# One tile's residual moved from a vector add to an accumulating transfer of GpSimd, in a hand-ordered end of an attention kernel

## The chip, the cores and the metric

The kernel runs on one core of one Trainium2 chip. The metric is the device time of one execution in microseconds (us). The engines are named as the profile names them: PE (matrix multiplications), DVE (VectorE), ACT (ScalarE), POOL (GpSimd) and SP (SyncE, which here only issues transfers).

## The reference

```python
def reference(A_x, A_wq, A_wk, A_wv, A_wo, B_x, B_w1, B_w2):
    x = A_x                                   # (1, 2048, 512), bfloat16
    xn = _layernorm(x, axis=-1)
    s = _A_ref(xn, A_wq, A_wk, A_wv, A_wo)    # attention, 32 query heads of 16, one k/v head; output projection wo
    g = _silu(_B_ref(xn, B_w1, B_w2))         # dense 512 -> 1792, silu, dense 1792 -> 512
    return x + s * g
```

## The kernel before

The 2048 rows are cut into four chunks of 512, and the 32 heads into groups of four, which makes 32 groups in order, eight to a chunk. For each group PE forms scores (line 643, and line 692 for the last group's parts) in PSUM banks psA, psD and psF. The exponential of some tiles is taken on ACT (`exp_A`, line 674, from psA to `pa_sb`), and of others as integer arithmetic on DVE (line 714) with shifted copies made by POOL with an int64 add (line 739). PE then multiplies both with v into psO (`emit_quad`, line 769): four matmuls over four column strips, a "quad". The feed-forward branch g is worked out in between and kept in `tmp_sb`.

The order of the instructions is written out by hand as two strings. `ORDER` is for the bulk. `TAIL`, read by `finish`, is for the end of the last group. A helper, `Sched`, puts each operation into its engine's queue in the order of the string, and derives the semaphore waits from the names of what it reads and writes. So a letter's place decides where an instruction stands in the queue of its own engine; letters of different engines that change places change nothing.

The last group's output for a few key blocks is worked out in three parts of its 512 rows: part 0 has rows 0 to 255, part 1 has 256 to 383, part 2 has 384 to 511. The letters of `TAIL`:

- `H`: eight (or four) score matmuls of one part on PE and their exponential on ACT
- `v`, and `q` with a part: one quad of PV on PE
- `n` with a part: the next of the part's four normalising steps on DVE: transpose from psO (line 920), reciprocal (923), product (872), transpose into `xn_sb` (929)
- `P`: four matmuls of the output projection of the next of the last chunk's four row tiles (line 404), for head groups that are already done; three to a tile, and the banks of tiles 0 to 3 are psF, the two halves of psD, and psA
- `r` with a tile: the last four matmuls of that projection, which need the part of the tile's rows (part 0 for tiles 0 and 1, part 1 for tile 2, part 2 for tile 3)
- `G`: bank times g on DVE, from PSUM (line 1429); or in two steps `C`, a copy on ACT out of PSUM (line 1424), and `M`, the product on DVE from SBUF (line 1426)
- `A`: the residual, an add of x on DVE into `ob_sb` (line 1444), and a store on SP's queue
- `X`, `Y`: the residual on PE by the identity matrix (line 1435); `Z`: its copy on ACT into `ob_sb` (line 1439) and a store on ACT's queue
- `a`: the residual by an accumulating transfer on POOL's queue, which adds the tile to the output in memory:

```python
op("gp", lambda e: e.dma_start(ov[:, tt, :], src, accum_op=ALU.add), reads=[key, "outx"], writes=[("out", tt)],
   lane=f"ac{tt % 4}", cost=3.0)
```

The output holds x already: one transfer copies all of it there early (line 397, `outx`). The tiles of the first three chunks are finished with such accumulating transfers (twelve in all, line 1122). At the start of `finish` POOL is given a small add on `mhalf_sb` (line 1398), before which its configuration is changed. At the end SP waits for all stores.

Of the kernel before, what the change touches and what calls it, by code (L numbers as in the profile page):

```python
# [213 lines left out]
def bass_recurrent_scan__grouped_kv_mqa__dense_activation_silu__prompt_kernel(  # L214
# [84 lines left out]
    TAIL = "vvHvvHvvHvvHq0q0q0q0q1q1q1q1n0PPn1Pn0n1q2q2q2q2n0Pn1n0Pn1Pn2r0r1C1n2G0PPPn2r2A0Pn2PM1PG2r3X1Y1Z1G3A2A3"  # L299
    ALPHA = "".join(chr(x) for x in range(35, 127) if x != 92) + "".join(chr(x) for x in range(192, 255))  # L300

    with ExitStack() as es:
# [1206 lines left out]
        while not followed:  # L1509
# [71 lines left out]
            else:  # L1581
                now = 0.0
        finish(TAIL)
        last = {}
# [36 lines left out]
```

## Time and profile before

| | us |
|---|---|
| median of 3 runs | 637.72 |
| lowest and highest run | 637.59, 638.5 |
| the profiled execution | 637.56 |
| its span | 635.8 |

The profile shows one execution. A row of the timeline gives the start in us from the span's start, the length in us, the engine, the line, the operation, output<-inputs and shapes, xN for N merged instructions, and in brackets how long the engine was idle before and what released it. PEld is PE's load of weights. For a transfer, the row's length is that of its issue; the time from issue to landing is given separately. The span's last 2.5 us show no instruction of a compute engine, only transfers.

### The profile page before, as it was taken

The numbers are of one execution on the slowest core, as the hardware profiler recorded it, in microseconds if no ns is written. First come the engines' busy times: TensorE is split into PE (matmuls) and PEld (weight loads), VectorE is DVE, ScalarE is ACT, GpSimd is POOL, SyncE is SP. The second block draws the span as 40 slices with busy tenths as digits, with TensorE's granted clock in tenths as the row PEclk, the third lists the DMA queues.
The fourth block names the chain that finished last, engine by engine and source line by source line (L and its number), as shares of the span: only waits on it lengthen the run. The fifth ranks groups of instructions, "written<-read, shape, count | busy, mean of one in ns | idle before, by whom it ended". The sixth has DMA issues, their size and how long they took to land.

```text
span 635.8 us, 18802 instructions
## 1 busy us (share of the span) xinstructions
PE 628.9 (99%) x8225; PEld 195.9 (31%) x8227; DVE 605.6 (95%) x1049; ACT 625.3 (98%) x721; POOL 436.4 (69%) x438
## 2 busy tenths in 40 slices
PE   8999999999999999999999999999999999999997
PEld 3433333332323222223223332223323233223323
DVE  7999999999999999999999999999999999999994
ACT  8999999999999999999999999999999999999996
POOL 6466665767667778767666876678767776776771
PEclk9999999999999999999999999999999999999999
DMA  6380000000000100000000000001000000000012
GB/s 183 119 283 2 2 2 2 2 3 1 2 2 2 19 1 11 10 2 2 1 3 2 1 3 2 2 10 18 10 3 2 2 2 1 3 1 2 3 18 53
DMA packets 10083, 12.51 MB, mean 20 GB/s; under 512 B 2288, under 2 KB 9456, under 8 KB 9968
## 3 DMA queue, kind: packets, MB, share of 16 engines
q1 hardware_dynamic: 7840, 9.34, 4.5%
q0 software_dynamic: 1728, 1.57, 2.2%
q8 instruction: 64, 1.05, 0.7%
q10 hardware_dynamic: 432, 0.39, 0.2%
q14 instruction: 19, 0.16, 0.1%
HBM read 8.95 MB, written 4.19 MB: 21 GB/s over the span
## 4 chain that ended last, share of the span: by engine, by line
PE 84%; ACT 9%; DVE 5%; issue 0%; DMA 0%; DVEq 0%
PE psO L769 32%; PE psA L643 27%; PE psF L404 20%; ACT pa_sb L674 8%; DVE ph_sb L714 3%; PE psD L643 2%; DVE x_sb L714 1%; ACT t_sb L1116 0%; PE psA L692 0%; DMA x_sb<-in_A_x_dram 0%; PE psD L507 0%; PE psD L476 0%; PE psF L643 0%; PE psD L533 0%; DVE stats_sb L424 0%
## 5 line engine op out<-in xcount | busy, mean ns | idle before, releaser
L674 ACT ACTIVATE pa_sb<-psA 128x1024 bf16<-128x1024 f32 x630 | 593.0, 1078 | 1.7 <-PE psA L643 0.6
L739 POOL INT64_ADD ph_sb<-ph_sb x304 | 317.1, 1058 | 131.0 <-DVE ph_sb L714 130.8
L714 DVE TENSOR_SCALAR ph_sb<-psD 128x512 int16<-128x512 f32 x521 | 336.3, 681 | 10.4 <-PE psD L643 8.5
L769 PE MATMUL psO<-ph_sb,vaug_sb 128*32 128x512 bf16 x1824 | 227.7, 383 | 0.1
L769 PE MATMUL psO<-pa_sb,vaug_sb 128*32 128x512 bf16 (+1 forms) x1292 | 201.6, 378 | 0.2 <-DVE rcp_sb L923 0.2
L643 PE MATMUL psA<-qT_sb,kTa_sb 32*128 32x512 bf16 x632 | 122.1, 384 | 0.1
L739 POOL INT64_ADD x_sb<-x_sb x90 | 93.5, 1057 | 41.4 <-DVE x_sb L714 41.3
L643 PE MATMUL psA<-qT_sb,kTb_sb 32*128 32x512 bf16 x612 | 118.4, 385 | 0.3 <-ACT pa_sb L674 0.3
L643 PE MATMUL psD<-qT_sb,kTb_sb 32*128 32x512 bf16 x335 | 113.5, 384 | 0.0
L643 PE MATMUL psD<-qT_sb,kTa_sb 32*128 32x512 bf16 x339 | 110.8, 385 | 0.0
L714 DVE TENSOR_SCALAR x_sb<-psD 128x512 int16<-128x512 f32 x153 | 100.7, 682 | 6.1 <-PE psD L643 5.3
L769 PE MATMUL psO<-x_sb,vaug_sb 128*32 128x512 bf16 x540 | 96.4, 383 | 0.0
L769 PEld LDWEIGHTS psO<-ph_sb,vaug_sb 128*32 128x32 bf16 x1824 | 55.6, 95 | 57.5 <-issue 35.1
L643 PEld LDWEIGHTS psA<-qT_sb,kTa_sb 32*128 32x128 bf16 x632 | 29.7, 91 | 122.0 <-ACT pa_sb L674 93.1
L404 PE MATMUL psF<-w_sb,u_sb 128*32 128x512 bf16 x896 | 66.2, 384 | 0.0
L643 PEld LDWEIGHTS psA<-qT_sb,kTb_sb 32*128 32x128 bf16 x612 | 28.7, 91 | 121.1 <-ACT pa_sb L674 99.2
L404 PE MATMUL psF<-xnT_sb,w_sb 128*32 128x512 bf16 x896 | 64.7, 383 | 0.0
L769 PEld LDWEIGHTS psO<-pa_sb,vaug_sb 128*32 128x32 bf16 x1292 | 50.2, 95 | 33.7 <-issue 24.2
L714 DVE TENSOR_SCALAR ph_sb<-psF 128x512 int16<-128x512 f32 x70 | 47.6, 680 | 0.0
L1116 ACT ACTIVATE t_sb<-psF 128x512 bf16<-128x512 f32 x72 | 46.3, 643 | 0.0
L1135 DVE SCALAR_TENSOR_TENSOR u_sb<-t_sb,psF 128x512 bf16<-128x512 bf16 x56 | 38.0, 678 | 0.2
L643 PEld LDWEIGHTS psD<-qT_sb,kTa_sb 32*128 32x128 bf16 x339 | 28.8, 91 | 2.2 <-DVE ph_sb L714 0.4
(120 smaller groups left out, 396.1 us busy)
## 6 DMA issues: line engine op xcount, KB each, us to landing
w_sb<-in_B_w_dram SPq DMA_DIRECT2D x2, 1792.0 KB, 10.9
x_sb<-in_A_x_dram SPq DMA_DIRECT2D x3, 512.0 KB, 5.6
out_dram<-ob_sb POOLq DMA_DIRECT2D x12, 128.0 KB, 3.1
wop_sb<-in_A_wo_dram SPq DMA_DIRECT2D x1, 512.0 KB, 4.0
wq_sb<-in_A_wq_dram SPq DMA_DIRECT2D x1, 384.0 KB, 5.9
out_dram<-ob_sb SPq DMA_DIRECT2D x3, 128.0 KB, 1.9
x_sb<-in_A_x_dram SPq DMA_DIRECT2D x2, 128.0 KB, 2.7
x_sb<-in_A_x_dram ACTq DMA_DIRECT2D x2, 128.0 KB, 2.9
```

Of the source, the lines that this page charges most:

```text
L404: r = e.matmul(bank[32 * i:32 * i + 32, :], lhsT=w, rhs=rhs, start=start, stop=stop, tile_position=(0, 32 * i), skip_group_check=True)
L643: return e.matmul(ap, lhsT=kT_sb[g % 2][32 * i:32 * i + 32, kt * P:(kt + 1) * P], rhs=qT_sb[32 * i:32 * i + 32, c % 2, g // 2, :], start=T ...
L674: d = op("a", lambda e: e.activation(pa_sb[:, sl, :], psA[k][:, :], ACT.Exp, scale=ESCALE), reads=["A%d" % k], writes=[("pa", sl)], cost=2 ...
L714: d = op("v", lambda e: e.tensor_scalar(ph_ap(0, sl, 512 * pos, 512 * pos + m), src, float(PH_ONE + PH_BIAS), 0.0, op0=ALU.add, op1=ALU.ma ...
L739: d = op("gp", lambda e, j=j: e.int64_add(ph_ap(j, sl, 0, 4 * NQ).bitcast(I64), ph_ap(0, sl, 0, 4 * NQ).bitcast(I64), PH_SHIFT[j] * 0x0001 ...
L769: r = e.matmul(psO[32 * i:32 * i + 32, cs], lhsT=vaug_sb[:, p["v"], p["kt"], DH * (gi % 2):DH * (gi % 2) + 32], rhs=p["ap"], start=s0, sto ...
L1116: d = op("a", lambda e: e.activation(t_sb[:, n % 2, :], bank_ap(b), ACT.Tanh, scale=0.5 if jb[0] == "h" else 0.25), reads=[b], writes=[("t ...
L1135: op("v", lambda e: e.scalar_tensor_tensor(out=dst, in0=t_sb[:, n % 2, :], scalar=1.0, in1=src, op0=ALU.add, op1=ALU.mult), reads=tk["read ...
```

## The change

The one string `TAIL` is replaced. Tile 0's residual was `A0` (add on DVE, store on SP) and is now `a0`, the accumulating transfer on POOL, from the scaled tile itself (`wq_sb`, whose space holds it by then). Tile 3's product with g was `G3` and is now `C3` and `M3`. The letters around them are in another order:

```diff
-    TAIL = "vvHvvHvvHvvHq0q0q0q0q1q1q1q1n0PPn1Pn0n1q2q2q2q2n0Pn1n0Pn1Pn2r0r1C1n2G0PPPn2r2A0Pn2PM1PG2r3X1Y1Z1G3A2A3"
+    TAIL = "vvHvvHPvvvvHHq0q0q0q0q1q1q1q1n0PPn1PPn0Pn1Pq2q2q2n0n1q2Pn0n1r1n2C1n2n2Pr2Pn2r0PPr3X1G2C3M1A2G0a0Y1M3Z1A3"
```

By engine, the queues before and after differ as follows from the second H on:

- PE: one P and four v stand between the second and third H, which is then followed at once by the fourth; six P instead of three stand between the quads of part 1 and those of part 2; after these it is P, r1, P, r2, P, r0, PP, r3, X1, Y1 instead of PPP, r0, r1, PPP, r2, PPP, r3, X1, Y1.
- DVE, after step 1 of part 2: step 2, step 3, G2, M1, A2, G0, M3, A3 instead of G0, step 2, A0, step 3, M1, G2, G3, A2, A3.
- ACT: C3 is added between C1 and Z1.
- POOL: the accumulating transfer of tile 0 is added behind the add on `mhalf_sb`, as the last entry of the queue.
- SP: two stores instead of three; the last is that of tile 3 in both.

## The prediction

> **What bounds the kernel now.** I read the page's head first, then the chain of waits that ended last, cut to its last microseconds, then the timeline of each engine there, and last the sources of the two kinds of transfer to the output.
>
> ```profile
> span 635.8 us, 18802 instructions
> PE 628.9 (99%) x8225; PEld 195.9 (31%) x8227; DVE 605.6 (95%) x1049; ACT 625.3 (98%) x721; POOL 436.4 (69%) x438
> ```
>
> PE, ACT and DVE are busy for nearly the whole span, and an edit of the tail string touches none of that: until the second of the last four H, at 624.63, both kernels issue the same instructions in the same order. Only the last 11 us can move, so a fault in my sum is a fraction of a microsecond, not a per cent.
>
> ```profile
> 626.86 0.80 PE psO L769 x32
> 628.48 0.41 PE psO L769 x16
> 629.80 0.04 DVE wq_sb L1429
> 632.55 0.41 DVE ob_sb L1444
> 632.95 0.34 DVEq L302
> ```
>
> These pieces (start, length, what) show the chain leaving PE when the last quads of part 2 are done (628.48 + 0.41 = 628.89), and running on DVE from there until the last residual add. What DVE does in that stretch is this, from its timeline (start, length, line, output<-inputs):
>
> ```profile
> 628.80 0.44 DVE L929 STREAM_TRANSPOSE xn_sb<-onb_sb 128x128 f32<-128x128 f32 x2
> 629.16 0.27 DVE L920 STREAM_TRANSPOSE otr_sb<-psO 128x128 f32<-128x128 f32 x1
> 629.47 0.18 DVE L923 RECIPROCAL rcp_sb<-otr_sb 128x4 f32<-128x4 f32 x1
> 629.80 0.69 DVE L1429 SCALAR_TENSOR_TENSOR wq_sb<-psF,tmp_sb 128x512 bf16<-128x512 f32 x1 [0.15 <-PE psF L404]
> 630.41 0.22 DVE L872 TENSOR_TENSOR onb_sb<-otr_sb,rcp_sb 128x64 bf16<-128x64 f32 x1
> 630.54 0.42 DVE L1444 TENSOR_TENSOR ob_sb<-wq_sb,x_sb 128x512 bf16<-128x512 bf16 x1
> 630.88 0.23 DVE L929 STREAM_TRANSPOSE xn_sb<-onb_sb 128x64 f32<-128x64 f32 x1
> 631.04 0.38 DVE L1426 TENSOR_TENSOR wq_sb<-wq_sb,tmp_sb 128x512 bf16<-128x512 bf16 x1
> 631.35 0.68 DVE L1429 SCALAR_TENSOR_TENSOR wq_sb<-psD,tmp_sb 128x512 bf16<-128x512 f32 x1
> 631.95 0.67 DVE L1429 SCALAR_TENSOR_TENSOR wq_sb<-psA,tmp_sb 128x512 bf16<-128x512 f32 x1
> 632.55 0.74 DVE L1444 TENSOR_TENSOR ob_sb<-wq_sb,x_sb 128x512 bf16<-128x512 bf16 x2
> ```
>
> From 629.80 to 632.55 + 0.74 = 633.29 DVE has no gap: G0, step 2 and A0, step 3, M1, G2, G3, A2, A3 in the letters of the string. What follows is the store of tile 3 on SP, read from the timeline and from the store's source:
>
> ```profile
> 632.98 0.82 SPq L1391 DMA_DIRECT2D out_dram<-ob_sb  x2
> L1391 SPq DMA_DIRECT2D out_dram<-ob_sb x2: 350/390/431, 633.0 to 633.4; - x2
> ```
>
> The last issue ends at 632.98 + 0.82 = 633.80 and took 0.43, so it began at 633.37, 0.08 after the add.
>
> **Part 1: part 2's scores are issued later (costs).** The new string puts one output projection (P) and four quads (v) between the second and the third of the four H, and the third and fourth H together.
>
> ```profile
> 624.28 0.38 PE L769 MATMUL psO<-pa_sb,vaug_sb 128*32 128x512 bf16 x1
> 624.63 0.40 PE L692 MATMUL psA<-qT_sb,kTb_sb 32*128 32x128 bf16 x8
> 624.96 0.39 PE L769 MATMUL psO<-ph_sb,vaug_sb 128*32 128x512 bf16 x1
> 625.18 0.38 PE L769 MATMUL psO<-pa_sb,vaug_sb 128*32 128x512 bf16 x1
> 625.55 0.40 PE L692 MATMUL psA<-qT_sb,kTb_sb 32*128 32x128 bf16 x8
> 626.47 0.40 PE L692 MATMUL psA<-qT_sb,kTb_sb 32*128 32x128 bf16 x8
> 627.00 1.25 ACT L674 ACTIVATE pa_sb<-psA 128x1024 bf16<-128x1024 f32 x1
> 586.38 1.94 ACT L674 ACTIVATE pa_sb<-psA 128x1024 bf16<-128x1024 f32 x2 [0.25 <-PE psD L643]
> ```
>
> Four column matmuls take 0.22 (624.96 to 625.18). Five such groups put the last at 624.96 + 4 x 0.22 = 625.84; back to scores takes 0.35 (624.28 to 624.63), so the third H starts at 626.19 instead of 625.55. Its matmuls end 0.40 later, and an exponential starts 0.13 after that (626.47 + 0.40 to 627.00): 626.72. The pair at 586.38 began on an idle ACT: 1.94 for both. So the fourth exponential ends at 626.72 + 1.94 = 628.66, where it ended at 627.00 + 1.25 = 628.25: 0.41 later. The fourth H still waits for the same exponential as before (626.47) and costs nothing more.
>
> **Part 2: PE behind it.**
>
> ```profile
> 627.46 0.82 PE L404 MATMUL psF<-wop_sb,xn_sb 128*32 128x512 bf16 x12
> 628.70 0.83 PE L404 MATMUL psD<-wop_sb,xn_sb 128*32 128x512 bf16 x12
> ```
>
> Six P instead of three now stand before the quads of part 2 (PP, PP, P, P), besides the one done already at 624.96. Six slots of 0.22 from 627.46 end at 628.78, just under the start of those quads, which is 0.23 after the exponential (628.25 to 628.48), thus 628.89. The P are therefore hidden by ACT; without that cover each would cost 0.22. The quads end at 628.89 + 0.41 = 629.30. DVE's next step used to start at 629.16 because DVE itself was busy with parts 0 and 1 until then (628.80 + 0.44 = 629.24, the steps overlap by some hundredths); now PE releases it, 0.05 after its end, at 629.35. So only 0.19 of the 0.41 reaches DVE.
>
> **Part 3: DVE is relieved (gains).** Part 2's four steps go first, each waiting for the one before with 0.03 between them: 629.35, 629.66, 629.87, 630.12, ending at 630.35 where they ended at 630.88 + 0.23 = 631.11. Then, by the start-to-start times of the rows above (0.16 after a step 3, 0.60 after a G, 0.31 after M1, 0.34 after an A): G2 630.28, M1 630.88, A2 631.19, G0 631.53, M3 632.13. A3 needs M3's result, 0.38 + 0.03 later: 632.54, ending 632.95. That is 0.34 before the old end: A0 has gone (0.34), G3 (0.60) has become M3 (0.41), against 0.19 lost at the start and the waits that nothing fills now.
> PE has the banks in time: after the quads P 629.11, r1 629.33, P 629.55, r2 629.77, which ends at 630.18, before G2; P, r0 at 630.21, long before G0; PP and r3 at 630.87, ending 631.28. The added copy C3 on ACT has the row of C1:
>
> ```profile
> 630.01 0.60 ACT L1424 ACTIVATE wq_sb<-psD 128x512 bf16<-128x512 f32 x1 [1.77 <-PE psD L404]
> ```
>
> 631.34 + 0.60 = 631.94, 0.19 before M3. Behind C3 on ACT wait Z1 and the store of tile 1; Y1, which waits for M1's end at 631.26, started 0.43 after it before, so Z1 starts near 632.1 and its store lands near 634.5, not last. SP loses one store and keeps A2's and A3's; A3's is issued at 632.95 + 0.08 = 633.03.
>
> **Part 4: the accumulating transfer (costs).** It replaces A0 and a store on SP. It is the last entry of POOL's queue, behind the add on mhalf; nothing waits behind it but the end.
>
> ```profile
> L1122 POOL DMA_DIRECT2D out_dram<-ob_sb x12: 850/869/1165, 210.5 to 622.5; - x12
> DMA to landing us min/median/max: 2.8/3.1/3.4
> DMA to landing us min/median/max: 1.9/2.0/2.0
> 421.20 0.68 DVE L1147 SCALAR_TENSOR_TENSOR ob_sb<-psF,tmp_sb 128x512 bf16<-128x512 f32 x1
> 422.18 0.87 POOL L1122 DMA_DIRECT2D out_dram<-ob_sb  x1 [1.20 <-DVE ob_sb L1147]
> 630.49 0.19 POOL L1398 TENSOR_TENSOR mhalf_sb<-mhalf_sb 128x4 f32<-128x4 f32 x1 [7.09 <-issue]
> 633.30:635.80 2.50, 0.00 (x0) 0.00 (x0) 0.00 (x0) 0.00 (x0) 0.00 (x0) 0.93 0.45 157
> ```
>
> The first landing row is the accumulate's, the second that of the last two plain stores. POOL starts 0.30 after DVE's result (421.20 + 0.68 to 422.18), and is free since 630.68. G0 ends at 631.53 + 0.68 = 632.21, so the transfer is issued at 632.51 and lands at 635.61 by the median of twelve (635.3 to 635.9 by their ends). It shares the DMA engines with A3's store. The end of before moved 157 GB/s at a share of 0.45, so about 350 GB/s when full (my estimate from that row); 128 KB are 0.37 us. Sharing costs between nothing and that; three plain stores overlapped in the old end without landing later than 2.0, so I take the low side, 0.1: landed at 635.71.
> The old end was 633.37 + 1.95 = 635.32, with 0.44 to the span's end at 635.76. A3's store would now land at 633.03 + 1.95 = 634.98, and the accumulate 0.7 after it. **Sum:** -0.34 on the old last store, then +0.73 because another transfer is last: 635.71 + 0.44 = 636.15, that is +0.4. The profiled execution took 637.56 outside and all; it becomes 637.96. The median before, 637.72, lies 0.16 above that execution, so the median after is **638.1**. About 0.2% (1.28 us) is what a measurement of this kernel can tell from no change, so this is a "same".
>
> **Rivals.**
> *Hidden transfer.* The accumulate lands before A3's store, which then sets the end: -0.34, 637.4. It decides from a landing time of 634.98 - 632.51 = 2.47 down; the fastest of twelve took 2.8, so against. The Trainium skill, "DMA: Bandwidth & Descriptors", section "Anatomy of one DMA — SWDGE (gpsimd) path", fits 2.0 us plus bytes over 436 GB/s for such a transfer, by which 128 KB would take about 2.3 us and this rival would win; the trace disagrees with its 3.1.
> *Locked out by DVE.* M3 and A3 run from 632.13 to 632.95, over the issue. If POOL can write nothing before A3 ends, the issue slips by 632.95 - 632.51 = 0.44, and the median after is 638.5; with a landing of 3.4 and full sharing it is 639.1. One old issue did overlap a DVE operation with two inputs:
>
> ```profile
> 454.20 0.73 DVE L872 TENSOR_TENSOR onb_sb<-otr_sb,rcp_sb 128x512 bf16<-128x512 f32 x1
> 454.58 0.88 POOL L1122 DMA_DIRECT2D out_dram<-ob_sb  x1 [0.52 <-DVE ob_sb L1147]
> ```
>
> It took 0.88 against 0.87, so against; but its inputs were f32, not bf16. The Trainium skill, "SBUF — State Buffer", section "SBUF: two separate sides", warns that DVE's two-port modes starve the descriptors of GpSimd's transfers; its section "Who interferes with whom" excepts tensor_tensor. By the warning this rival holds, by the exception my sum.
> *POOL not ready (slower).* All twelve old accumulates were issued between int64 adds. This one comes after POOL's change of configuration, which kept it for 7.09 us until 630.49. If the transfer needs such a change again, it starts at 630.68, ends at 637.77, and the landing comes at 640.9: the span ends at 641.3, a median of 643.3. It decides from 0.9 us of extra delay, where the result passes +0.2%. Against it: the first accumulate, at 210.5, came in the middle of adds and shows no such gap, only an issue of 1.17 at most.
>
> **How the numbers follow.** My forecast has 0.60, the hidden transfer 0.12, the lockout 0.14, POOL not ready 0.14 (with any long first start there). The range runs from the hidden transfer, less 0.1 for the spread of the runs, 637.3, to the lockout's upper end, 639.2; it leaves out POOL not ready. Slower by over 0.2% (over 639.0) has that 0.14, a third of the lockout, and 0.04 of the forecast where landing and sharing are both at their worst and H comes later than I have it: 0.23. Faster by over 0.2% would need a landing before 634.0, which no case reaches; 0.04 for what I have not seen. The same: 0.73.
>
> **What would show it.** In the new profile: the last L674 ending near 628.65; L929 of part 2 ending near 630.35; the last L1444 near 632.95; a POOL L1122 starting near 632.5 and landing near 635.7, last of all. It is wrong if SP's last wait is for the plain store, if the POOL row starts late, or if DVE shows a gap before the second L1426 (then C3 was late).

## The result, and the profile after

| us | before | after |
|---|---|---|
| median of 21 runs each, side by side | 638.42 | 639.40 |
| lowest and highest | 637.50, 639.37 | 638.33, 640.82 |
| the profiled execution | 637.56 | 639.53 |
| its span | 635.8 | 637.7 |

The ratio is 1.0016, with a 95% interval of 1.0009 to 1.0022: the changed kernel is slower by about 1.0 us. The middle value is within 0.2%, but the whole interval lies above 1, and the loss is about 2.5 times the 0.4 us forecast. The 639.4 also lies above the range, whose upper end was 639.2. Part of that has nothing to do with the change: the median of before is 638.42 over 21 runs, 0.70 above the 637.72 of three runs that the prediction started from. On that base the measured +0.98 would have given 638.70, inside the range.

The profiled executions differ by 1.97 us, and half of this is not in the end at all. These are the `L692` rows of the first of the last four H before, and of the first and second in the changed kernel:

```profile
623.72 0.40 PE L692 MATMUL psA<-qT_sb,kTb_sb 32*128 32x128 bf16 x8
```

```profile
624.63 0.40 PE L692 MATMUL psA<-qT_sb,kTb_sb 32*128 32x128 bf16 x8
625.55 0.40 PE L692 MATMUL psA<-qT_sb,kTb_sb 32*128 32x128 bf16 x8
```

So 0.91 us were lost ahead of any instruction that the change moves. A second profile of each kernel (last experiment) has that stretch the other way round, so it scatters between executions. Everything below is therefore read from the first of the four H. Its time to the span's end is called the tail here; ends and landings are taken from the trace to the nanosecond. The tail was 12.05 us before and is 13.10 us after, +1.05, which agrees with the medians' +0.98.

The chain of waits of the changed kernel, its last pieces (start, length, what):

```profile
630.95 0.25 DVE xn_sb L929
631.20 0.02 DVE wq_sb L1429
631.22 0.48 issue
631.69 0.40 DVE wq_sb L1426
632.10 0.33 DVE ob_sb L1444
632.43 0.61 DVE wq_sb L1429
633.04 0.29 issue
633.33 1.05 POOL out_dram L1122
```

Before, the chain ended with the last `L1444` on DVE. Now it leaves DVE after G0 (`L1429` at 632.43) and ends in POOL's issue of the accumulating transfer. The timeline of the same stretch:

```profile
627.07 0.70 PE L692 MATMUL psA<-qT_sb,kTb_sb 32*128 32x128 bf16 x16
627.51 1.94 ACT L674 ACTIVATE pa_sb<-psA 128x1024 bf16<-128x1024 f32 x2 [0.18 <-PE psA L692]
630.12 0.32 DVE L920 STREAM_TRANSPOSE otr_sb<-psO 128x128 f32<-128x128 f32 x1
630.95 0.25 DVE L929 STREAM_TRANSPOSE xn_sb<-onb_sb 128x64 f32<-128x64 f32 x1
631.12 0.65 DVE L1429 SCALAR_TENSOR_TENSOR wq_sb<-psD,tmp_sb 128x512 bf16<-128x512 f32 x1
632.35 0.69 DVE L1429 SCALAR_TENSOR_TENSOR wq_sb<-psF,tmp_sb 128x512 bf16<-128x512 f32 x1
632.95 0.42 DVE L1426 TENSOR_TENSOR wq_sb<-wq_sb,tmp_sb 128x512 bf16<-128x512 bf16 x1
633.33 1.05 POOL L1122 DMA_DIRECT2D out_dram<-wq_sb  x1 [1.55 <-DVE wq_sb L1429]
633.40 0.42 DVE L1444 TENSOR_TENSOR ob_sb<-wq_sb,x_sb 128x512 bf16<-128x512 bf16 x1
633.85 0.35 SPq L1391 DMA_DIRECT2D out_dram<-ob_sb  x1
```

DVE ends at 633.40 + 0.42 = 633.82, which is 632.91 on the scale of before (less 0.91), and 0.38 earlier than the 633.29 there. So DVE did gain. What comes after it is seen in three more views: the source of the accumulate (line 1122, its last instance), the source of the closing instructions (line 302), and SP's waits, all of the changed kernel.

```profile
L1122 POOL DMA_DIRECT2D out_dram<-wq_sb x1: 1055/1055/1055, 633.3 to 633.3; - x1
DMA to landing us min/median/max: 3.6/3.6/3.6
L302 POOLq DRAIN  x1: 3917/3917/3917, 633.6 to 633.6; - x1
L302 ACTq DRAIN  x1: 155/155/155, 633.6 to 633.6; - x1
L302 SPq DRAIN  x1: 7/7/7, 637.1 to 637.1; - x1
L302 SPq EVENT_SEMAPHORE  x1: 17/17/17, 637.7 to 637.7; - x1
SPq L302 <- DMA out_dram<-wq_sb: 0.7, 1, 0.7
SPq L302 <- PEq L302: 0.6, 1, 0.6
```

And of before, the rows that answer to them:

```profile
L302 POOLq DRAIN  x1: 10349/10349/10349, 621.4 to 621.4; - x1
L302 SPq DRAIN  x1: 7/7/7, 635.5 to 635.5; - x1
L302 SPq EVENT_SEMAPHORE  x1: 17/17/17, 635.7 to 635.7; - x1
SPq L302 <- PEq L302: 0.2, 1, 0.2
```

The transfer lands 3.60 us after its issue began, at 633.33 + 3.60 = 636.93. Then comes something that the prediction did not have. POOL's queue ends with a closing instruction, DRAIN, which every engine has. Before, it ended at 621.4 + 10.35 = 631.7, long before the end. Now it ends at 637.51, which is 0.57 after the landing. SP is done with its own DRAIN at 637.1 and then waits 0.6 us instead of 0.2 (the view names PE's queue, whose part was long done; the last DRAIN to end is POOL's). From the landing to the span's end there are 0.80 us, where before there were 0.46 from the last store's landing. So of the 1.05 us, 0.72 are the later last landing (12.30 of the tail against 11.59) and 0.34 the longer closing. Not every engine's DRAIN waits in this way: ACT's took 0.15 and was over 1.8 us ahead of the landing of ACT's own store (9.13 against 10.94 of the tail).

### The profile page after: what moved, and what is told of

It is laid out like the page before. It is cut to its first block, busy times and chain, and to the rows that moved or that the text cites. A ratio compares the mean times of both kernels' runs of the same rounds, so it can differ in the third digit from the quotient of the medians.

```text
span 637.7 us, 18802 instructions
## 1 busy us (share of the span) xinstructions
PE 630.1 (99%) x8227; PEld 196.3 (31%) x8227; DVE 606.3 (95%) x1048; ACT 626.0 (98%) x722; POOL 436.2 (68%) x439
## 3 DMA queue, kind: packets, MB, share of 16 engines
q8 instruction: 64, 1.05, 0.7%
## 4 chain that ended last, share of the span: by engine, by line
PE 83%; ACT 9%; DVE 6%; DMA 0%; issue 0%; POOL 0%; SPq 0%
PE psO L769 32%; PE psA L643 27%; PE psF L404 20%; ACT pa_sb L674 8%; DVE ph_sb L714 3%; PE psD L643 2%; DVE x_sb L714 1%; ACT t_sb L1116 0%; DMA x_sb<-in_A_x_dram 0%; DVE onb_sb L872 0%; PE psA L692 0%; PE psD L507 0%; PE psD L476 0%; PE psF L643 0%; PE psD L533 0%
```

## The experiments

Each row: the places where POOL's transfer and the store of tile 3 begin to be issued, counted from the first of the four H, the time from there to landing, the tail, and the ratio to the time of before where there are enough runs for one. Tails and landings are those of one profile each.

| kernel | POOL's transfer | tile 3's store | tail | ratio [95%] |
|---|---|---|---|---|
| before | none | 9.66 + 1.93 | 12.05 | |
| before, second profile | none | 9.66 + 1.94 | 12.06 | |
| after | 8.71 + 3.60 | 9.22 + 2.30 | 13.10 | 1.0016 [1.0009, 1.0022] |
| after, second profile | 8.71 + 3.56 | 9.23 + 2.43 | 13.08 | |
| order alone | none | 9.69 + 2.16 | 12.31 | 0.9995 [0.9986, 1.0004] |
| transfer alone | 7.08 + 3.27 | 9.49 + 2.03 | 11.98 | 1.0002 [0.9993, 1.0010] |
| transfer and M3 | 7.15 + 3.24 | 9.57 + 1.99 | 12.02 | 0.9999 [0.9991, 1.0008] |
| early accumulate | 7.30 + 3.08 | 9.10 + 2.56 | 12.12 | 1.0002 [0.9993, 1.0011] |
| late small transfer | 9.87 + 2.47 | 9.66 + 1.93 | 13.15 | 1.0012 [1.0003, 1.0021] |
| small transfer first | 8.76 + 3.41 | 9.27 + 1.70 | 13.01 | |
| two stores less | 8.71 + 3.28 | none | 12.79 | |
| both of these | 8.71 + 3.08 | none | 12.63 | |
| no change of configuration | 8.71 + 3.47 | 9.23 + 3.11 | 12.99 | |
| early plain add | none | 9.30 + 2.34 | 12.41 | 1.0004 [0.9995, 1.0013] |

### Which part of the change costs: the order, or the transfer

The new order with tile 0's old add and store in it:

```diff
-…Pr2Pn2r0PPr3X1G2C3M1A2G0a0Y1M3Z1A3
+…Pr2Pn2r0PPr3X1G2C3M1A2G0A0Y1M3Z1A3
```

> The new order with tile 0's residual left on DVE and SP (A0 in place of a0). I time the end from the first 128-column score matmul of line 692 to the span's end: 12.05 us before, 13.10 after. Theory T (the accumulating transfer, coming last, costs the microsecond: it lands late and POOL's closing drain comes after it): the transfer is gone, DVE is 0.4 longer than after, and the end is 12.0 to 12.3, a time within 0.3 us of before. Theory O (the new order costs it, by the later scores of part 2 or by a busier end of DVE): the end stays at 12.8 to 13.4, a time about 1 us above before.

Measured: 638.29 against 638.52, ratio 0.9995 [0.9986, 1.0004], tail 12.31. The order by itself makes no difference that this measurement can tell, and it doesn't carry the 1.0 us. Its one tail is 0.26 longer than before, nearly all of it in a slower landing of tile 3's store (2.16 against 1.93).

The other half, the old order with the transfer in place of the add:

```diff
-…r1C1n2G0PPPn2r2A0Pn2PM1PG2r3X1Y1Z1G3A2A3
+…r1C1n2G0PPPn2r2a0Pn2PM1PG2r3X1Y1Z1G3A2A3
```

> The old order with tile 0's residual by the accumulating transfer (a0 in place of A0), which is then issued near the end of G0, some 1.7 us earlier than after. Theory T in its place-bound form (the transfer costs only because it comes last): it lands by 634.6 on before's scale, POOL's drain ends before the last plain store lands at about 635.0, DVE is 0.34 shorter, and the end is 11.6 to 11.8 us instead of 12.05. Rival form (an accumulate after POOL's change of configuration costs about a microsecond wherever it stands, by a drain of 3 us or more from its issue): the end is 12.3 or more. Theory O: no loss, 11.6 to 12.1.

Measured: 638.7 against 638.52, ratio 1.0002 [0.9993, 1.0010], tail 11.98. The accumulate now has its place early, behind the old early G0:

```profile
630.97 1.06 POOL L1122 DMA_DIRECT2D out_dram<-wq_sb  x1
632.52 0.75 DVE L1444 TENSOR_TENSOR ob_sb<-wq_sb,x_sb 128x512 bf16<-128x512 bf16 x2
SPq L302 <- PEq L302: 0.2, 1, 0.2
```

Its landing still takes 3.27 us, and yet it costs nothing: POOL's DRAIN ends at 10.92 of the tail, ahead of the last store's landing at 11.52, and SP's last wait is back at 0.2. The gain is small as well, and the tail misses the 11.6 to 11.8 expected. Removing A0 brought tile 3's store forward by 0.17 only, where A0 had been priced at 0.34: it stood in part in a gap that DVE has anyway, since from the product of part 2 to its last transpose there are 0.48 us with A0 and still 0.26 without it. Of the 0.17, 0.10 went into a slower landing.

The same with G3 split into C3 and M3, as the change has it:

```diff
-…r2A0Pn2PM1PG2r3X1Y1Z1G3A2A3
+…r2a0Pn2PM1PG2r3X1Y1C3Z1A2M3A3
```

> The old order with a0 in place of A0, and tile 3's product as C3 and M3 behind A2 in place of G3. By the rows of before, DVE ends another 0.13 us sooner than with a0 alone, if the copy C3 on ACT is done in time: an end of 11.5 to 11.7 us and about 0.5 us under before under theory T. If C3, which now stands ahead of Z1, makes tile 1's store the last one, 11.8 or more.

Measured: 638.4 against 638.52, ratio 0.9999 [0.9991, 1.0008], tail 12.02. The shorter DVE operation brought nothing either, where 0.13 was expected: M3 had to wait for C3 (done at 632.22, M3 at 632.25), and tile 3's store was issued 0.08 later than with the transfer alone. So neither half of the change costs the 1.0 us alone; the intervals reach up to 0.3 us for the order and 0.6 us for the transfer. In the two together the accumulate comes last.

### Is it the lateness of the transfer

The new order with r0, G0 and a0 brought forward, ahead of the steps of part 2:

```diff
-…n0n1q2Pn0n1r1n2C1n2n2Pr2Pn2r0PPr3X1G2C3M1A2G0a0Y1M3Z1A3
+…n0n1q2Pn0n1r0n2r1C1n2G0a0n2Pr2Pn2PPr3X1G2C3M1A2Y1M3Z1A3
```

> The new order with r0, G0 and a0 moved forward: r0 on PE right after part 2's quads, G0 and a0 between steps 1 and 2 of part 2; the rest of DVE then is step 2, step 3, G2, M1, A2, M3, A3. Theory T (place of the transfer decides): the accumulate is issued near 7.2 us from the first 128-column matmul of line 692 and lands near 10.5, its drain is over by 11.1, the last plain store is issued near 9.2 to 9.3 (before 9.66) and lands near 11.2, and the end is 11.6 to 11.8 us against 12.05 before and 13.10 after, a time 0.3 to 0.4 us under before. Theory O (the new order itself is slow): 12.3 or more.

Measured: 638.11 against 637.82, ratio 1.0002 [0.9993, 1.0011], tail 12.12. Of the 1.05 us, 0.98 are gone when the same transfer, in nearly the same order, is issued 1.4 us earlier. What did not come is the gain (a tail of 11.6 to 11.8 was expected), though tile 3's store was issued 0.56 earlier than before. From the source of the stores (line 1391), here and before:

```profile
DMA to landing us min/median/max: 2.4/2.4/2.6
```

```profile
DMA to landing us min/median/max: 1.7/1.8/2.0
```

Tile by tile the three stores land 0.4 to 0.7 us later after their issue than before, and the 0.63 of tile 3's gives back the 0.56.

Then the closing DRAIN by itself. The kernel before, with a plain transfer of 512 B from one scratch tile to itself on POOL's queue, behind tile 3's add, for which nothing waits but the end:

```diff
+            op("gp", lambda e: e.dma_start(scr_sb[:, 2:4], scr_sb[:, 0:2]), reads=[("ob", 3), "scr", "scr1"], writes=["scrw"],
+               lane="late", cost=3.0)
```

> The kernel before, with one more transfer on POOL, 512 bytes of scratch to scratch, issued when the last residual add is done. Nothing waits for it, SP neither, and every other instruction stands where it stood. Theory drain: POOL does not finish before it has landed, 0.57 us after that: issue at 9.87 us from the first 128-column matmul of line 692, landing 1.86 later (as the small transfer of the warm run), drain over at 12.3, end of the span at 12.5 instead of 12.05, about 0.5 us in the time. Rival: a transfer that nobody waits for costs nothing: 12.05.

Measured: 638.81 against 637.82, ratio 1.0012 [1.0003, 1.0021], tail 13.15. From the timeline, the sources and SP's waits:

```profile
633.23 0.43 SPq L1391 DMA_DIRECT2D out_dram<-ob_sb  x1
633.44 0.74 POOL L1448 DMA_DIRECT2D scr_sb<-scr_sb  x1 [2.53 <-DVE ob_sb L1444]
DMA to landing us min/median/max: 2.5/2.5/2.5
L302 POOLq DRAIN  x1: 2791/2791/2791, 633.7 to 633.7; - x1
SPq L302 <- PEq L302: 1.3, 1, 1.3
```

The stores are those of before (tile 3's at 9.66, landing after 1.93), and the kernel is nevertheless slower by about what the change costs. A transfer of no size and no use on POOL's queue, if it is the last to land, ends the kernel 0.80 after its own landing (12.35 to 13.15). It took 2.47 us to land instead of the 1.86 expected, and so the tail came out above the expectation. A transfer has landed when all 16 increments of its semaphore have come; here the fifteenth came 1.94 after the issue and the last 0.54 later, so about half of the 1.1 us that the tail grew is this increment and not the closing (more of this below). The DRAIN ended 0.57 after the landing again.

This 0.57 is what tells two readings of the DRAIN apart. If it lasted a fixed time from the end of the issue, it would not move with the landing. From the issue's end to the DRAIN's end there are 3.12 us in the changed kernel, 2.79 with the transfer alone and 2.31 here, while from the landing to the DRAIN's end there are 0.57 to 0.61 in every one of these runs.

### Why 3.6 us and not 3.1

The prediction took the median of the twelve earlier accumulates. Two things plainly differ at the end: the transfer is the first after POOL's change of configuration, and it runs beside three stores. First a small transfer ahead of it, which takes the first place:

```diff
             op("gp", lambda e: e.tensor_tensor(mhalf_sb[:, :], mhalf_sb[:, :], mhalf_sb[:, :], ALU.add), reads=["mhalf"], writes=["mhalf"])
+            op("gp", lambda e: e.dma_start(scr_sb[:, 2:4], scr_sb[:, 0:2]), reads=["scr", "scr1"], writes=["scrw"], lane="warm", cost=3.0)
```

> The kernel after, with one small plain transfer on POOL (512 bytes of scratch) right behind the add on mhalf, some 1.5 us ahead of a0. It changes nothing of the output. After, a0's issue took 1.06 us against a median of 0.87, its first packet came 1.76 us after its start against 1.43, and it landed after 3.6 us against 3.0. Theory cold (the first transfer after POOL's change of configuration is slow to start): the small one takes that delay, a0's issue is back at 0.85 to 0.90 and its landing 0.2 to 0.4 us shorter. Theory crowd (M3, A3 and the stores beside it slow it): issue 1.0 or more and landing 3.5 or more, as after.

Measured: 639.48, tail 13.01. The issue took 0.91 instead of 1.05, and the landing 3.41 instead of 3.60. The first packet did not come earlier for it (10.49 of the tail against 10.47).

Then the changed kernel without the stores of tiles 1 and 3, which are not written out:

```diff
-                    store("a" if a == "Z" else "sp", k)
+                    if k not in (1, 3):
+                        store("a" if a == "Z" else "sp", k)
```

(and the same at the store of `A`)

> The kernel after without the stores of tiles 1 and 3 (their rows of the output keep x alone; nothing else is left out). The accumulate then shares the DMA engines only with tile 2's store, issued 0.9 us before it. Theory crowd: part of its slow landing (3.6 us from issue against 3.0 in the median) is the two stores beside it; the time from the end of its issue to its first packet goes back from 0.71 to about 0.57, the landing to 3.2 to 3.4. Rival (the delay is its own, from the cold start of its issue): 3.55 or more. Theory drain (POOL's closing drain ends a fixed 0.57 us after the accumulate has landed, as in the three runs with one): the drain follows the landing. Rival (the drain takes a fixed 3.1 us from the end of the issue): it stays 3.1 behind the issue whatever the landing does.

Measured: 639.07, tail 12.79. The issue is as long as in the changed kernel, 1.05, and the landing comes after 3.28, the first packet at 10.33. With both edits at once:

> The changed kernel with both earlier edits at once: the small plain transfer of 512 B on GpSimd's queue ahead of the accumulate, and no stores of tiles 1 and 3 (these two tiles are not written out). One edit alone brought the landing of the accumulate from 3.60 us after its issue to 3.41 (small transfer first) and 3.28 (two stores less), and the median of the twelve earlier accumulates is 3.1. Theory (two separate causes that add: a long issue behind the change of configuration, and company of the last stores): issue 0.86 to 0.92 us, first packet 0.57 us behind the issue's end, landing 3.05 to 3.2 us from the issue, tail 12.55 to 12.7 us. Rival (the shorter issue is paid back by a later first packet, which stood 0.82 us behind the issue's end with the small transfer): landing 3.25 us or more, tail 12.75 us or more.

Measured: 638.18 against 637.60 in the one run beside it, tail 12.63. The last instance of line 1122, and the DRAIN:

```profile
L1122 POOL DMA_DIRECT2D out_dram<-wq_sb x1: 916/916/916, 632.4 to 632.4; - x1
DMA to landing us min/median/max: 3.1/3.1/3.1
L302 POOLq DRAIN  x1: 3725/3725/3725, 632.4 to 632.4; - x1
```

The four landings are 3.60, 3.41, 3.28 and 3.08. The small transfer goes with 0.19 and 0.20, the two stores with 0.32 and 0.33, whichever of the two comes first, and with both edits the transfer is one like the twelve. From the landing to the end of this last run there are 0.85.

These sums look like two causes that add, but the trace shows a third difference between the same runs. In the changed kernel the fifteenth increment came 3.35 after the issue began and the last 0.25 later (3.34 and 0.22 in the second profile). In the other three the last was 0.07, 0.04 and 0.02 behind. The changed kernel also has an 8 KB transfer of the queue that the DMA view calls "instruction" at 9.66 to 10.26 of the tail, on top of the stores' packets. With the small transfer ahead none stands there, and without the two stores it is over at 10.03, ahead of the accumulate's first packet. So of the 0.40 between 3.60 and the forecast 3.2, 0.25 stand with one late increment. How much of the rest is the longer issue and how much the stores beside it is not separated: the early accumulate had an issue of 1.04 and landed after 3.08 all the same.

Last, is the long issue due to the change of configuration or to DVE, which runs M3 and A3 beside it? The changed kernel without the add on `mhalf_sb`, before which the configuration is changed:

> The kernel after without the add on mhalf at the end of POOL's queue, and so without the change of POOL's configuration ahead of it; the result is the same, POOL only ends in another configuration. Theory cold: a0's issue goes from 1.06 us back to 0.85 to 0.90 and the landing shortens by about 0.2. If the issue stays at 1.0 or more, the change of configuration has nothing to do with it, and M3 and A3 on DVE beside it are the suspects. POOL's drain 0.57 behind the landing as before, if it has nothing to do with the configuration either.

Measured: 646.35 against 637.82, tail 12.99. From the sources and the start of POOL's timeline:

```profile
L1122 POOL DMA_DIRECT2D out_dram<-wq_sb x1: 862/862/862, 639.8 to 639.8; - x1
L353 POOLq MODIFY_POOL_CONFIG  x2: 11/11/11, 1.2 to 1.2; - x2
9.69 0.28 POOL L353 TENSOR_SCALAR_AFFINE_SELECT ident<-ident 128x128 bf16<-128x128 bf16 x1 [8.76 <-issue]
```

The issue is back at 0.86 beside the same M3 and A3, so its length came with the configuration and not from DVE. The landing came after 3.47, only 0.13 sooner, where 0.2 was expected; POOL's DRAIN ended 0.57 behind it. The first of the twelve accumulates is also the first transfer after a change of configuration (line 605, at 23.5 us); its issue took 1.17, and it landed after 3.18. The time was 7.0 us over the changed kernel's 639.40, and this is not in the tail. The new execution has its own change of configuration at 1.2 us (the L353 row), as every kernel here has. Behind it POOL waits 8.76 us for nothing that the profile shows, where it waited 0.50 in the kernel before (the same instruction stood at 1.43 there). So the change is paid at the start if it isn't made at the end, where POOL had nothing else to do.

### What is left of the gain without the transfer

If it is the accumulate's packets that delay the stores in the early version, the same order with the plain add (one step of part 2 further back than `a0`) should keep the earlier store:

```diff
-…n0n1r0n2r1C1n2G0a0n2Pr2Pn2PPr3X1G2C3M1A2Y1M3Z1A3
+…n0n1r0n2r1C1n2G0n2A0Pr2Pn2PPr3X1G2C3M1A2Y1M3Z1A3
```

> The order of the run with the early accumulate, but with the plain addition A0 in the transfer's place: the first tile's residual comes forward of the exponentials' quads (right behind G0) and no transfer of GpSimd is left in the end. Theory (the crowding by the accumulate's packets is what held the last store's landing at 2.56 us there): A3's store is issued 9.3 to 9.4 us behind the first 128-column score multiplication and lands within 2.0 us, tail 11.7 to 11.9 us against 12.05 before, the kernel 0.15 to 0.35 us under the one before. Rival (a late increment on one DMA engine strikes the stores in any order, or the DVE's order gains nothing): the store lands after 2.2 us or more, tail 12.1 us or more, and the time is within 0.1 us of before or above it.

Measured: 638.68 against 638.56, ratio 1.0004 [0.9995, 1.0013], tail 12.41. By its own signs the theory falls. Tile 3's store was issued at 9.30 as expected, but landed after 2.34, and tile 1's store on ACT's queue landed last, at 11.81 of the tail, 2.56 after its issue.

The increments tell two kinds of delay apart, though. Here 15 of the 16 of tile 3's store had come 1.93 after its issue, and the last of each of these two stores was 0.41 late. Had it not been, the tail would be about 11.86 by my estimate (the fifteenth of tile 1's at 11.40, and 0.46 to the end), which is what the theory expected. In the early version no increment stood out: the fifteenth of tile 3's store came after 2.50 and the last after 2.56. So the accumulate's packets remain the likelier cause there, and what this run met is another disturbance.

That disturbance goes together with the "instruction" queue. In fourteen profiles the tail's transfers with a last increment of over 0.2 late (0.22 to 0.92) are all in five: both of the changed kernel, the order alone, the late small transfer and this one. In these five an 8 KB transfer of that queue falls on their packets or on those just ahead of them (from 9.55 to 10.13 here). In the others it is over, or not there, when such packets run; in both profiles of before it ends at 9.39 and 9.85, and the first packets of the last three stores come at 10.05. This was not tested, and what sets the time of that transfer stays open.

### How much two profiles of one kernel differ

> The kernel before unchanged, for a second profile of it: tail from the first 128-column score multiplication to the span's end 12.0 to 12.1 us, as in the first profile, if the tail scatters little; the stretch ahead of it within 0.3 us of 623.72.

> The changed kernel unchanged, for a second profile of it. Theory (the accumulate's landing and GpSimd's closing drain set the end): tail 12.8 to 13.2 us, the drain ending 0.57 us behind the transfer's landing, the transfer landing 3.3 to 3.6 us from its issue. The stretch ahead of the tail is 0.9 us longer than before in the first profile; if that belongs to this execution alone, it falls back to within 0.3 us of 623.72, and if it belongs to the changed code, it stays at about 624.6.

Measured: tails 12.06 and 13.08, within 0.03 of the first profiles; landing 3.56, DRAIN 0.57 after it. The first of the four H stands at 624.87 in the second profile of before and at 624.40 in that of after:

```profile
624.87 0.40 PE L692 MATMUL psA<-qT_sb,kTb_sb 32*128 32x128 bf16 x8
```

```profile
624.40 0.40 PE L692 MATMUL psA<-qT_sb,kTb_sb 32*128 32x128 bf16 x8
```

So neither expectation for the stretch ahead of the tail was met as written: before was not within 0.3 of 623.72, and after lies between its two cases. The 0.91 by which after was later in the first pair is -0.47 in the second. The bulk scatters by about a microsecond between executions, and the tail by hundredths, which is why differences of tails say more here than differences of spans.

## Why the prediction was wrong, step by step

It had the sign of the tail's change and part of its mechanism, an accumulate that lands last. What failed are two terms of Part 4: the landing, and the time from the landing to the end. All numbers of after are here less 0.91, on the scale of the prediction.

- **Part 1** held. The third H started at 626.16 (forecast 626.19). The exponentials ended at 628.53, not 628.66, so that 0.28 of the 0.41 came.
- **Part 2** held. The added P were hidden by ACT. DVE's first step of part 2 started at 629.21 (629.35).
- **Part 3** held within 0.1: steps done at 630.28 (630.35), G2 630.21 (630.28), G0 from 631.44 to 632.12 (631.53 to 632.21), M3 632.04 (632.13), A3's end 632.91 (632.95). There was no gap ahead of M3, so C3 on ACT was in time.
- **Part 4**, the start, held: issue at 632.42 (632.51).
- **Part 4**, "lands at 635.61 by the median of twelve" and "three plain stores overlapped in the old end without landing later than 2.0, so I take the low side, 0.1", failed. It landed after 3.60 instead of 3.2, at 636.02 instead of 635.71. The twelve were not like it: their median of 3.07 is met (3.08) only with a small transfer ahead and two stores less. Of the 0.40, 0.25 stand with one late increment; the split of the rest stays open, as said above. Plain stores beside plain stores were a poor row for the price of sharing: two stores less went with 0.32, where 0.1 had been put. An accumulate keeps the DMA engines busy for longer than such a store, as the DMA view of the changed kernel from 630 us to the end shows (packets, MB, share of 16 engines' time):

```profile
q0 software_dynamic: 144, 0.13, 14.1%
q10 hardware_dynamic: 144, 0.13, 4.7%
```

The first row is the accumulate, the second one plain store with as many bytes in as many packets. The accumulate's packets took three times as long: 14.1% of 7.73 us is 1.09 us of all 16 engines, against 0.36 for the store, for which I had put 0.37.

- **Part 4**, "nothing waits behind it but the end" and "+ 0.44" to the span's end, failed. That end is itself an instruction in POOL's queue, the DRAIN. The 0.44 was read where POOL had been done for 4 us and was carried over to a case in which POOL is last. It is 0.80: 0.36 more. The run with the late small transfer shows this term by itself, since nothing else was changed there.

By these, +0.40 becomes +0.40 - 0.09 (earlier issue) + 0.40 (landing) + 0.36 (closing) = +1.07; measured were +1.05 in the tail. The rest of the miss, from 638.1 to 639.4, is the 0.70 in the median that it started from. The signs of being wrong that the prediction named (a plain store last, a late POOL row, a gap ahead of M3) did not appear; none of them looked at what comes behind the landing.

**The rivals.** The hidden transfer fell: 3.60 against the 2.47 it needed. The Trainium skill's fit in "DMA: Bandwidth & Descriptors", section "Anatomy of one DMA — SWDGE (gpsimd) path", by which 128 KB would take about 2.3 us (an estimate), is short of every accumulate measured here: the fastest of the twelve took 2.83, and the one at the end with both edits 3.08. The lockout by DVE fell: the issue started while M3 ran, and took 0.86 in the run without the change of configuration, beside the same operations. This agrees with the exception for tensor_tensor that the Trainium skill makes in "SBUF — State Buffer", section "Who interferes with whom". POOL not ready, with 7 us more, fell too; of its idea only the longer issue is true (1.05 against 0.86 without the change of configuration). The loss that came was none of these three; it lay in two terms of the forecast itself.

## What to carry to other kernels

A transfer on POOL's queue near the end cost more than its landing here, because POOL's closing instruction came behind it, while ACT's did not wait for ACT's store. So see in the profile which engine's DRAIN ends last, and take the time from landing to span's end from a case in which that engine was last. A typical landing from the bulk of a kernel can be too low for one at the end, where stores crowd together (3.07 against 3.60 here); look at single increments before you give the difference a cause. In this kernel the accumulating transfer was free of cost only where it was issued early, and there it saved little: taking out DVE's add brought the last store forward by half of the add's price.

## What the runs showed of the hardware

- POOL's closing DRAIN ended 0.57 to 0.61 us after the landing of its queue's last transfer, in all runs that have one in the tail, whatever its size (512 B or 128 KB). ACT's, of 0.15 us, did not wait for the landing of ACT's store; SP's took 0.01 us behind SP's own wait for the stores.
- The first transfer of POOL after the change of configuration was issued in 1.04 to 1.06 us, a later one in the same place in 0.91 to 0.92, and one without the change in 0.86.
- An accumulating transfer of 128 KB took three times the DMA engines' time of a plain store of 128 KB (1.09 us of all 16 against 0.36). Beside it stores landed after 1.7 us where their packets came first (10.13 against 10.49 of the tail, with the small transfer ahead), and after 2.0 to 3.1 where the accumulate's came first (the transfer alone, the transfer and M3, the early version, and no change of configuration, where tile 3's took 3.11). Stores as late as 2.63 also came without an accumulate (the order alone), so it is not the only cause.
- In the tails of fourteen profiles, a last increment of a transfer that came 0.2 to 0.9 us behind the other 15 was seen only where an 8 KB transfer of the "instruction" queue ran on or just ahead of its packets.
- The change of configuration that the kernel makes at its end costs some 8 us of POOL's time at the start of the next execution if it is left out, 7.0 us of the whole in the one run.
